# Attention and MLP in one launch: when two items' heads are loaded, and which PSUM banks the stages get

## The chip, the cores and the metric

The kernel runs on one core of one Trainium2 chip. The metric is the device time of one launch in microseconds, the median of several runs. A core has five engines that run side by side, each with its own queue of instructions, worked off in order: PE (TensorE, matrix products), DVE (VectorE), ACT (ScalarE), POOL (GpSimd) and SP (SyncE, which here issues every DMA). They wait for each other on semaphores. PE writes its products into PSUM, which has eight banks of 128 partitions by 512 float32 numbers.

## The reference

One transformer block on 2048 rows of width 512, float32:

```
x  = A_x                                          # 2048 x 512
qkv = layernorm(x) @ wqkv                         # 32 heads of 16 columns each
p  = softmax(q @ k^T / 4)                         # per head, 2048 x 2048
h  = x + (p @ v) @ wo
h2 = h + silu(layernorm(h) @ w1) @ w2             # inner width 1792
```

## The kernel before, in words

**Items.** Attention is cut into 32 items: item `i` is the block of 512 queries number `i // 8` with the four heads `4 * (i % 8)` and up, so the first eight items are all heads of the first 512 queries. For an item the four heads' keys (`ks`, all 2048) and queries (`qs`, the item's 512) lie in SBUF in one of `RING = 5` buffers. `load_k(i, k)` and `load_q(i, k)` (L196 to L205) each issue one DMA for one head, from the DRAM tensors `kd` and `qd`. `HEADS[k]` gives a head's place as a pair (a, j); half `j` of the partitions holds two heads.

**Maxima.** The softmax subtracts an upper bound of each row's maximum, which is computed exactly: `maximum` (L216) makes a 128 x 512 tile of scores on PE (`ps_m`) and DVE reduces it to 128 maxima (`mx`, L225). An item has 64 such tiles. `one_max` (L297) does the next one of the list: the halves `j` alternate, and within a half the first four tiles are of one head, the next four of the other. `burst(n)` does n of them. When an item's 64 are done, `finish_max` combines them on POOL, and three units later `place_max` (L254) turns the result on PE (`ps_n`), copies it on ACT (`mt`) and sends it by two DMAs into two rows of `qs`.

**Three stages and their banks.** `open_banks` (L133) opens PSUM pools; a bank of a newly opened pool that lies where banks of a closed pool lay is released by the last readers of the closed pool's tiles.

- Stage 0 (pools st of 3 banks and sm of 5): layer norm, the values of all rows, and queries and keys of the first two items. It ends with a burst of five maxima.
- Stage 1 (L578 to L607, pools st of 2 and sm of 6): the *late projections*, 24 units of 12 products each. `project_qk` (L406) makes 128 columns (eight heads, two items) of queries or keys for one block of 512 rows, in a bank of pool st. In the middle of the 12 products it calls a burst of six maxima, which use pool sm. Then ACT scales the bank into `scaled[b]` (in the profile `ks<-ps_qk`) and casts that to `sh` (three buffers), POOL makes the remainder `sl` (two buffers), and SP writes `sh` twice and `sl` once to `kd` or `qd`, in two DMAs. In the text the units have the code's number `n`, from -4 to 19. Units -4 to -1 are the keys of the third and fourth item (items 2 and 3), units 0 to 3 their queries; units 4 to 19 are those of items 4 to 7. The heads of items 2 and 3 are loaded in units 0 to 3. The last two units, 18 and 19, also start the first scores of attention (`begin_scores`) by the table `BESIDE_T`.
- Stage 2 (L611 on, pools st of 4, pv of 1, sm of 3): attention with the MLP of a finished block of rows between. Per group PE makes four tiles of scores (`ps_s`), ACT the exponentials (`pt`), PE the products with the values (`pv`), and up to three maxima of later items go beside them.

**What sets the order.** Every engine's order is the order of the calls (`keep_in_program_order`). SP is one queue for all DMAs: a DMA whose data isn't there, or whose buffer isn't free, holds up all behind it. The DMAs take eight semaphores in turn (called places here), so a DMA is issued only when the one eight before it has landed.

Of the kernel before, what the change touches and what calls it, by code (L numbers as in the profile page):

```python
# [77 lines left out]
def attention_mlp_kernel(ctx: ExitStack, tc: tile.TileContext, x, wqkv, wo, w1, w2, out):  # L78
# [25 lines left out]
    def dma(*a):  # L104
        pin(nc.sync.dma_start(*a))
# [27 lines left out]
    def open_banks(scope, n, **sizes):  # L133

        for kind, bufs in sizes.items():
            banks[kind] = scope.enter_context(tc.tile_pool(name=f"ps_{kind}{n}", bufs=bufs, space=PSUM))

    def bank(name, kind="st", dtype=F32):
        return banks[kind].tile([P, 512], dtype, tag=kind, name=name)
# [56 lines left out]
    def load_k(i, k, lo=0, n=S):  # L196
        a, j = HEADS[k]
        h = 4 * (i % 8) + 2 * a + j
        dma(ks[i % RING][64 * j:64 * j + 48, a, lo:lo + n], kd[:, h * DH:(h + 1) * DH, lo:lo + n])

    def load_q(i, k):
        a, j = HEADS[k]
        h = 4 * (i % 8) + 2 * a + j
        lo = i // 8 * 512
        dma(qs[i % RING][64 * j:64 * j + 48, a, :], qd[:, h * DH:(h + 1) * DH, lo:lo + 512])  # L205

    def fixed_rows(i):
        for j in range(2):
            r = 64 * j + 48
            dma(qs[i][r:r + 16], fix_q[:, None, :].to_broadcast([16, 2, 512]))  # L210
            dma(ks[i][r:r + 16].rearrange("p a (m n) -> p (a m) n", n=512),
                fix_k[:, None, :].to_broadcast([16, 8, 512]))
# [66 lines left out]
    def tick():  # L279
        at["step"] += 1  # L280
        for fn, a in agenda.pop(at["step"], ()):
            fn(*a)
# [14 lines left out]
    def one_max(half=None, ps=None):  # L297

        i = next_item()
        if i == ITEMS:  # L300
            return
        if half is None:
            half = at["half"]
            at["half"] = 1 - half
        if at["blocks"]:

            i = min(range(2), key=lambda n: (todo[n, half] or todo[n, 1 - half] or [(n, KC)])[0][1])
        elif not todo[i, half] and 64 * (i + 2) <= at["ready"] and KC * i - at["next"] > 12:

            i += 1  # L310
        half = half if todo[i, half] else 1 - half
        at["done"] += 1
        if maximum(*todo[i, half].pop(0), ps):
            steps = due_at(i)
            soon(steps, place_max, i, finish_max(i, at["group"] is not None and steps == WAIT))

    def burst(n, *more):
        for ps in more:
            one_max(ps=ps)
        for _ in range(n - len(more)):  # L320
            one_max()
# [16 lines left out]
    def scores(g, k, kind="st"):  # L338

        i, c = divmod(g, KC)  # L340
        a, j = HEADS[k]
        assert i in placed
        ps = bank("ps_s", kind)
        mm(ps, ks[i % RING][64 * j:64 * j + 64, a, c * P:(c + 1) * P], qs[i % RING][64 * j:64 * j + 64, a, :],
           start=True, stop=True)
        pts[g, k] = pt_tile("pt")
        act("activation", pts[g, k], ps, AF.Exp, scale=qk_f)


    with ExitStack() as pa:  # L350
# [55 lines left out]
        def project_qk(b, n, beside={}, scale=False):  # L406

            g, key = divmod(n, 2)
            cols = slice(key * D + g * P, key * D + (g + 1) * P)
            ps = bank("ps_qk")  # L410
            weave(product(ps, lambda c: wqk_h[:, c, cols], lambda c: wqk_l[:, c, cols],
                          lambda c: xth[b][:, c, :], lambda c: xtl[b][:, c, :], DC),
                  {k: n if callable(n) else (lambda n=n: burst(n)) for k, n in beside.items()})
            sh = xp.tile([P, 512], F16, name="sh")
            sl = xp.tile([P, 512], F16, name="sl", bufs=2)
            if scale:

                t = scaled[b]
                act("mul", t, ps, qk_s)
                act("copy", sh, t)  # L420
                pool("tensor_tensor", sl, t, sh, ALU.subtract)
            else:
                act("mul", sh, ps, qk_s)
                dve("scalar_tensor_tensor", sl, ps, qk_s, sh, op0=ALU.mult, op1=ALU.subtract)
            d = (kd if key else qd)[:, g * P:(g + 1) * P, b * 512:b * 512 + 512]
            hs, ls = (slice(0, 3, 2), 1) if key else (slice(0, 2), 2)
            dma(d[hs].rearrange("s d n -> d s n"), sh[:, None, :].to_broadcast([P, 2, 512]))
            dma(d[ls], sl)
# [152 lines left out]
        def begin_scores(n):  # L581

            for _ in range(n):
                g, k = first_scores.pop(0)
                scores(g, k, "sm")
                one_max(1 - HEADS[k][1])


        BESIDE_T = {3: lambda: begin_scores(3), 9: lambda: begin_scores(3)}, {3: lambda: (begin_scores(2), burst(2))}
        at["blocks"] = False  # L590
        open_banks(pa, 1, st=2, sm=6)

        pools.append(ctx.enter_context(tc.tile_pool(name="bp0", bufs=EARLY, side="right")))
        for g in range(1, NG // 2):
            for m, (b, key) in enumerate([(b, 1) for b in range(NB)] + [(b, 0) for b in range(NB)]):
                tick()
                if g == 1 and m < 2:
                    fixed_rows(2 + m)
                n = 8 * g + m - 12
                beside = {BESIDE_A1[m]: 6} if g == 1 and m < len(BESIDE_A1) else BESIDE_A  # L600
                if n >= 18:
                    beside = BESIDE_T[n - 18]
                project_qk(b, 2 * g + key, beside, True)
                if 0 <= n < 4:
                    for h in (n % 2 * 2, n % 2 * 2 + 1):
                        load_q(2 + n // 2, h)
                        load_k(2 + n // 2, h)  # L607

    open_banks(ctx, 2, st=4, pv=1, sm=3)  # L611
    pv = bank("pv", "pv")
    cpool = ctx.enter_context(tc.tile_pool(name="cpool", bufs=1, side="right"))
    bp = ctx.enter_context(tc.tile_pool(name="bp", bufs=PTS - EARLY))
# [369 lines left out]
    def maxima(g):  # L984

        i, c = divmod(g, KC)
        ready = min(ITEMS, i + RING - (0 if c == KC - 1 else 1)) * 64
        rate = max([(64 * (n + 1) - sum(x for x, m in zip(BESIDE, marks) if g <= m <= KC * n) - at["done"])
                    / max(1, KC * n - AHEAD - g) for n in range(i + 1, ITEMS)] or [0])
        if ready < END:  # L990
            rate = min(rate, (ready - at["done"]) / (KC - 1 - c or KC))
        at["due"] += max(0, rate)
        if g < LAG or g in marks or g - 1 in marks:

            return 0
        at["ready"] = ready
        most = 2 if c == JOINT and i and i - 1 not in FIRSTS else 3
        n = max(0, min(most, int(at["due"]), ready - at["done"]))
        at["due"] -= n
        return n  # L1000
# [3 lines left out]
    for g in range(groups):  # L1004
        tick()
        i, c = divmod(g, KC)
# [9 lines left out]
        if i in FIRSTS:  # L1016
            b, n = i // 8 - 1, c - OUTPUT
# [21 lines left out]
        n = maxima(g)  # L1039
# [48 lines left out]
```

## Time and profile before

| | us |
|---|---|
| median of 3 runs | 1687.23 (1686.25 to 1687.6) |
| the profiled execution | 1686.74 |
| its span, first to last instruction | 1685.0 |
| PE busy | 1661.9 (99%) |
| DVE busy | 1452.2 (86%) |
| ACT busy | 1240.0 (74%) |
| POOL busy | 283.8 (17%) |

Stage 0 ends near 95 us of the span, the late projections run from there to about 197 us, and attention and the MLP fill the rest. The page's busy share of PE counts overlapping instructions once, so 99% leaves some 23 us in which PE ran nothing. In rows of the timeline the columns are start, duration, engine, line, operation, output and input, shape and count; in brackets is the idle time before, with what ended it. Neighbouring instructions of one kind are merged, and the count is then over 1 (a merged row spans from its first start to its last end). Matmuls overlap: a 512-column product lasts 0.39 us in its row, while the next one starts 0.23 us after it.

### The profile page before, as it was taken

What the parts mean: (1) busy time and instruction counts of PE and PEld (TensorE: products, weight loads), DVE (VectorE), ACT (ScalarE), POOL (GpSimd) and SP (SyncE); (2) the same over time, 40 slices, a digit from 0 to 9 for tenths busy, and PEclk for the clock granted to TensorE, in tenths of its full rate; (3) what the DMA queues carried; (4) which work ended last, traced back from release to release, by engine and by line L of the source; (5) the groups of instructions that cost most, each with busy time, mean ns of one, the idle gap of its engine ahead of it and who ended that gap; (6) DMA issues with size and microseconds to landing.
All of it is one profiled execution on the core that took longest, in us unless ns stands there. A gap on an engine that the chain in (4) does not pass through costs nothing.

```text
span 1685.0 us, 28415 instructions
## 1 busy us (share of the span) xinstructions
PE 1661.9 (99%) x10542; PEld 650.2 (39%) x10542; DVE 1452.2 (86%) x2422; ACT 1240.0 (74%) x2441; POOL 283.8 (17%) x450
## 2 busy tenths in 40 slices
PE   9998999999999999999999999999999999999999
PEld 7665422222245532222245542222245542222387
DVE  7897999999978889999988889999978889997343
ACT  5322699999963279999963369999963379999743
POOL 5422310000033310000033310000034310000000
PEclk9999999999999999999999999999999999999999
DMA  5533411121223111111222211111222211100222
GB/s 179 125 87 129 120 43 39 37 50 38 64 59 88 60 49 32 37 49 39 62 60 80 69 50 31 37 45 43 60 61 80 70 49 32 35 11 21 64 75 82
DMA packets 100763, 102.83 MB, mean 61 GB/s; under 512 B 19092, under 2 KB 77524, under 8 KB 100624
## 3 DMA queue, kind: packets, MB, share of 16 engines
q1 hardware_dynamic: 100624, 101.01, 20.7%
q8 instruction: 83, 1.36, 0.3%
q14 instruction: 56, 0.46, 0.1%
HBM read 77.72 MB, written 17.29 MB: 56 GB/s over the span
## 4 chain that ended last, share of the span: by engine, by line
PE 85%; ACT 9%; DVE 3%; DMA 2%; issue 1%; POOL 0%; SPq 0%; ACTq 0%; DVEq 0%
PE pv L85 33%; PE ps_s L85 19%; PE ps_m L85 10%; PE ps_acc L85 10%; ACT pt L99 8%; PE ps_qk L85 4%; PE ps_wo L85 3%; PE ps_w L85 3%; PE ps_v L85 2%; DVE mx L225 1%; DMA ks<-kd 1%; PE ps_tr L88 1%; DMA ks<-in_A_x_dram 1%; DMA qd<-sh 0%; DVE pvs L102 0%
## 5 line engine op out<-in xcount | busy, mean ns | idle before, releaser
L225 DVE TENSOR_REDUCE mx<-ps_m 128x1 f32<-128x512 f32 x2009 | 1257.5, 682 | 92.6 <-PE ps_m L85 66.2
L99 ACT ACTIVATE pt<-ps_s 128x512 f32<-128x512 f32 x2048 | 1012.3, 608 | 19.0 <-PE ps_m L85 12.8
L85 PE MATMUL ps_s<-qs,ks 64*128 64x512 f16 x2048 | 534.0, 379 | 5.8 <-ACT pt L99 2.4
L85 PE MATMUL pv<-pt,va 128*17 128x512 f32 x4096 | 537.4, 598 | 1.2
L85 PE MATMUL ps_m<-ks,qs 48*128 48x512 f16 x2009 | 504.8, 380 | 6.2 <-ACT mt L99 3.2
L85 PEld LDWEIGHTS <-ks 64*128 64x128 f16 x2048 | 148.6, 94 | 542.2 <-issue 434.9
L85 PEld LDWEIGHTS pv<-pt,va 128*17 128x17 f32 x4096 | 68.7, 95 | 225.9 <-issue 208.3
L85 PEld LDWEIGHTS <-qs 48*128 48x128 f16 x2048 | 118.1, 94 | 73.9 <-issue 69.3
L99 ACT CAST w2h<-w 128x512 fp32r<-128x512 f32 x56 | 34.7, 620 | 102.0 <-PE ps_acc L85 102.0
L99 ACT ACTIVATE g<-pv 128x512 f32<-128x512 f32 x39 | 23.3, 597 | 102.2 <-PE pv L85 102.2
L85 PE MATMUL ps_acc<-w2l,gh 128*128 128x512 f32 x224 | 92.8, 415 | 0.0
L85 PE MATMUL ps_acc<-w2h,gh 128*128 128x512 f32 x224 | 92.4, 413 | 0.0
L85 PE MATMUL ps_acc<-w2h,gl 128*128 128x512 f32 x224 | 88.1, 393 | 0.0
L92 POOL TENSOR_TENSOR w2l<-w,w2h 128x512 fp32r<-128x512 f32 x42 | 53.8, 1281 | 164.7 <-ACT w2h L99 164.6
L102 DVE TENSOR_TENSOR gl<-g,gh 128x512 fp32r<-128x512 f32 x53 | 37.0, 699 | 46.7 <-ACT gh L99 46.7
L99 ACT ACTIVATE ks<-ps_qk,qk_s 128x512 f32<-128x512 f32 x30 | 20.7, 689 | 70.7 <-PE ps_qk L85 68.6
L92 POOL TENSOR_SCALAR nm<-nm 128x16 f32<-128x16 f32 x51 | 12.9, 253 | 327.1 <-DVE nm L235 323.8
L92 POOL TENSOR_TENSOR mx<-mx 128x32 f32<-128x32 f32 x38 | 9.5, 250 | 340.6 <-DVE mx L225 339.1
L85 PE MATMUL pv<-htl,w1h 128*128 128x512 f32 x156 | 65.6, 420 | 0.0
L92 POOL TENSOR_TENSOR ot<-ot,den 128x512 f32<-128x512 f32 (+1 forms) x16 | 20.4, 1273 | 256.3 <-DMA den<-dr 217.1
L85 PE MATMUL pv<-hth,w1h 128*128 128x512 f32 x156 | 62.5, 401 | 0.0
L85 PE MATMUL pv<-hth,w1l 128*128 128x512 f32 x156 | 61.4, 393 | 0.0
(130 smaller groups left out, 1409.4 us busy)
## 6 DMA issues: line engine op xcount, KB each, us to landing
w<-in_B_w_dram SPq DMA_DIRECT2D x112, 256.0 KB
ks<-kd SPq DMA_DIRECT2D x120, 192.0 KB
qs<-qd SPq DMA_DIRECT2D x128, 48.0 KB
kd<-sh SPq DMA_DIRECT2D x16, 256.0 KB
qd<-sh SPq DMA_DIRECT2D x16, 256.0 KB
hx<-in_A_x_dram SPq DMA_DIRECT2D x16, 256.0 KB
ot<-pvs SPq DMA_DIRECT2D x124, 32.0 KB
den<-dr SPq DMA_DIRECT2D x124, 32.0 KB
```

The lines of the kernel that those rows point to most:

```text
L85: tc.keep_in_program_order(nc.tensor.matmul(*a, **k))
L88: tc.keep_in_program_order(nc.tensor.transpose(*a))
L92: tc.keep_in_program_order(getattr(nc.gpsimd, op)(*a, **k))
L99: pin(getattr(nc.scalar, fn)(*a, **k))
L102: pin(getattr(nc.vector, fn)(*a, **k))
L225: pin(nc.vector.tensor_reduce(mx[i][:, j, a, qt, kb:kb + 1], ps, axis=AX.X, op=ALU.max))
```

## The change

Three edits, all in and around the late projections. `load_k` and `load_q` of items 2 and 3 are called in another order and in seven units in place of four. The pools of stage 1 are opened sm first, so sm takes banks 0 to 5 and st banks 6 and 7 (before: st 0 and 1, sm 2 to 7); those of stage 2 are opened st, sm, pv, so sm takes banks 4 to 6 and pv bank 7 (before: pv 4, sm 5 to 7). In the last unit the two scores and two maxima beside the products follow its first product in place of its third. Nothing is added or removed; PE, DVE, ACT and POOL keep their instructions and, but for those two products, their order.

```diff
+        loads = {0: ((load_k, 2, 0), (load_k, 2, 1)), 1: ((load_q, 2, 0), (load_q, 2, 1), (load_k, 2, 2)),
+                 2: ((load_q, 2, 2), (load_k, 2, 3), (load_q, 2, 3))}
+        for h in range(4):
+            loads[3 + h] = (load_k, 3, h), (load_q, 3, h)
+
-        BESIDE_T = {3: lambda: begin_scores(3), 9: lambda: begin_scores(3)}, {3: lambda: (begin_scores(2), burst(2))}
+        BESIDE_T = {3: lambda: begin_scores(3), 9: lambda: begin_scores(3)}, {1: lambda: (begin_scores(2), burst(2))}
         at["blocks"] = False
-        open_banks(pa, 1, st=2, sm=6)
+        open_banks(pa, 1, sm=6, st=2)
...
                 project_qk(b, 2 * g + key, beside, True)
-                if 0 <= n < 4:
-                    for h in (n % 2 * 2, n % 2 * 2 + 1):
-                        load_q(2 + n // 2, h)
-                        load_k(2 + n // 2, h)
+                for load, i, h in loads.get(n, ()):
+                    load(i, h)
...
-    open_banks(ctx, 2, st=4, pv=1, sm=3)
+    open_banks(ctx, 2, st=4, sm=3, pv=1)
```

SP's order around the loads, from the two programs, with `k2,0` for the keys of the third item's head with number 0 in `HEADS`, and `W(n)` for the two writes of unit n:

```
before: W(0) q2,0 k2,0 q2,1 k2,1 | W(1) q2,2 k2,2 q2,3 k2,3 mt mt | W(2) q3,0 k3,0 q3,1 k3,1 | W(3) q3,2 k3,2 q3,3 k3,3 | W(4) W(5) W(6) mt mt W(7)
after:  W(0) k2,0 k2,1 | W(1) q2,0 q2,1 k2,2 mt mt | W(2) q2,2 k2,3 q2,3 | W(3) k3,0 q3,0 | W(4) k3,1 q3,1 | W(5) k3,2 q3,2 | W(6) k3,3 q3,3 mt mt | W(7)
```

## The prediction

> **What bounds the kernel now.** I read the page's busy shares first, then the windows by stage, the waits, the timelines of PE, SP, ACT and DVE around the late projections, and the chain that ended last there.
>
> ```profile
> PE 1661.9 (99%) x10542; PEld 650.2 (39%) x10542; DVE 1452.2 (86%) x2422; ACT 1240.0 (74%) x2441; POOL 283.8 (17%) x450
> ```
>
> PE is the bound, so the change pays or costs where PE stands idle or runs slowly. Windows of 20 us show where that is (window, length, then busy time of PE, its weight loads, DVE, ACT, POOL, then granted clock, DMA share, GB/s):
>
> ```profile
> 100.00:120.00 20.00, 20.00 (x95) 12.30 (x94) 19.85 (x35) 7.31 (x12) 7.88 (x14) 1.00 0.45 115
> 120.00:140.00 20.00, 17.88 (x81) 11.26 (x80) 15.39 (x27) 5.79 (x10) 6.00 (x13) 0.91 0.27 95
> 140.00:160.00 20.00, 16.78 (x75) 10.73 (x73) 14.64 (x24) 5.39 (x9) 5.33 (x5) 0.91 0.40 141
> ```
>
> From 100 to 120 us PE and DVE are both full, so neither has room to hide a delay of the other. From 120 to 160 us PE loses 5.34 us and the clock falls to 0.91. PE's timeline has the bursts of maxima, one per unit (units 3 to 8 here, but for unit 6, whose burst is undisturbed), and what stood before them:
>
> ```profile
> 124.36 0.83 PE L85 MATMUL ps_m<-ks,qs 48*128 48x512 f16 x6
> 128.06 0.82 PE L85 MATMUL ps_m<-ks,qs 48*128 48x512 f16 x5
> 131.00 0.37 PE L85 MATMUL ps_m<-ks,qs 48*128 48x512 f16 x1 [2.12 <-DVE mx L225]
> 132.31 0.63 PE L85 MATMUL ps_qk<-xtl,wqk_h 128*128 128x512 f32 x1
> 132.74 0.63 PE L85 MATMUL ps_qk<-xth,wqk_h 128*128 128x512 f32 x1
> 135.85 0.82 PE L85 MATMUL ps_m<-ks,qs 48*128 48x512 f16 x6
> 143.65 0.61 PE L85 MATMUL ps_m<-ks,qs 48*128 48x512 f16 x4
> 147.48 0.39 PE L85 MATMUL ps_m<-ks,qs 48*128 48x512 f16 x2 [3.22 <-ACT mt L99]
> 152.33 0.82 PE L85 MATMUL ps_m<-ks,qs 48*128 48x512 f16 x6
> ```
>
> An undisturbed unit takes 3.70 us (124.36 to 128.06). Unit 4 to 5 takes 7.79, unit 7 to 8 takes 8.68: 4.09 and 4.98 lost, 9.07 us together. Each loss is a stall (2.12 and 3.22 us) and, after it, products that start 0.43 us apart (132.31 to 132.74).
>
> SP's timeline shows why. A DMA is issued when the one eight places before it has landed, so some issues mark landings:
>
> ```profile
> 117.92 0.33 SPq L105 DMA_DIRECT2D qd<-sl  x1
> 119.80 0.77 SPq L105 DMA_DIRECT2D qs<-qd  x1
> 126.61 1.26 SPq L105 DMA_DIRECT2D ks<-kd  x1
> 135.13 0.71 SPq L105 DMA_DIRECT2D ks<-kd  x1
> 138.36 0.67 SPq L105 DMA_DIRECT2D ks<-kd  x1
> 142.68 0.67 SPq L105 DMA_DIRECT2D ks<-kd  x1
> 145.95 0.34 SPq L105 DMA_DIRECT2D kd<-sl  x1
> ```
> ```profile
> 120.75 5.84 DMA ks<-kd
> 126.61 11.73 DMA ks<-kd
> 139.13 7.42 DMA qd<-sh
> ```
>
> In the chain, the load of keys k2,0 takes 5.84 us, k2,3 takes 11.73, and the write W(3) of unit 3 takes 7.42: one backlog. The stall of unit 4 ends at 131.0 when k2,1 has landed (DVE, the named releaser, had long been done); that of unit 7 when W(3) has landed at 146.55, since ACT's cast `sh` of unit 6 needs its buffer and the copy `mt`, whose bank the burst needs, stands behind the cast:
>
> ```profile
> 146.65 0.62 ACT L99 CAST sh<-ks 128x512 f16<-128x512 f32 x1 [3.96 <-DMA qd<-sh]
> ```
>
> **The loads.** Prices of the backlog, from the rows above: a pair of keys and queries 3.27 us (142.68, landing of k3,0, to 145.95, landing of k3,1), which by size (192 and 48 KB) is 2.62 and 0.65; two writes, a pair and the two `mt` 4.32 (138.36 to 142.68); two writes and a pair 4.13 (131.00 to 135.13), so two writes 0.86 and two `mt` 0.19. The second load of keys is dearer: 126.61 to 131.00 is 4.39, less 0.65 for q2,1 3.74.
>
> Sixteen loads and their instructions stay, so the backlog's content is unchanged; its order isn't. With PE undisturbed until then, k2,0 is issued right behind W(0)'s second write (117.92 + 0.33, near 118.3) and not behind that write's landing. It lands at 118.3 + 5.84 = 124.1, k2,1 at 127.9, W(1) at 128.7, q2,0 at 129.4, q2,1 at 130.0. Unit 4's sixth maximum needs k2,1 and q2,1 at 128.7: a stall of 1.3 in place of 2.12. Then k2,2 132.7, `mt` 132.9, W(2) 133.7, q2,2 134.4, k2,3 137.0, q2,3 137.7. The ninth tile of item 2, second in unit 6's burst, needs these; it would stand at 128.06 + 2 x 3.70 = 135.5. So both stalls together shift PE by 2.2 us. I take 2.2. Below, if the second keys cost 2.62 as later ones do, everything is 1.1 earlier and the shift is 1.1; above, the 9.07 of before.
>
> Behind W(3) the backlog now comes after the write and not before it: W(3) lands near 138.5, while unit 6, whose burst stands at 137.7 by now, has six products and a scale to go before its cast wants the buffer; so `mt` isn't late and the stall of unit 7 goes. What is late next: the writes of units 4 to 7 land 4.13 us apart, the casts come 3.70 apart, so the margin of some 2 us shrinks by 0.43 a unit and is just about used up at W(7), the last with a load ahead of it; a cast that came late there would delay no `mt` copy, as none stands there. POOL's remainders, with two buffers, come later still and wait for nothing that PE needs before unit 12. Item 3's heads are first needed in unit 15 (one tile in unit 4, then six a unit), past 170 us; with four times 0.86 + 3.27 behind 137.7 they land by 154. So the loads gain 9.07 - 2.2 = 6.9.
>
> **The first bank of stage 1.** Here the change adds a wait.
>
> ```profile
> 94.73 0.82 PE L85 MATMUL ps_m<-ks,qs 48*128 48x512 f16 x5
> 95.48 0.50 PE L85 MATMUL ps_qk<-xth,wqk_h 128*128 128x512 f32 x1
> 97.42 0.39 PE L85 MATMUL ps_qk<-xtl,wqk_h 128*128 128x512 f32 x1
> 97.65 0.39 PE L85 MATMUL ps_qk<-xth,wqk_h 128*128 128x512 f32 x1
> 98.29 0.82 PE L85 MATMUL ps_m<-ks,qs 48*128 48x512 f16 x6 [0.25 <-DVE mx L225]
> 101.78 1.08 PE L85 MATMUL ps_m<-ks,qs 48*128 48x512 f16 x6
> ```
> ```profile
> 94.42 3.82 DVE L225 TENSOR_REDUCE mx<-ps_m 128x1 f32<-128x512 f32 x6
> ```
>
> Before, unit -4's first product took a bank of the old st pool and waited for ACT's copy of values, long done: it starts at 95.48, ten products hide DVE's last reduces of stage 0 (to 94.42 + 3.82 = 98.24), and the burst waits only 0.25. Now st lies in banks 6 and 7, which the old sm pool held, and in the changed program this product waits for the last of those reduces, though the bank itself was reduced earlier. All of PE stands behind it: its start moves from 95.48 to 98.29, 2.81 later, less the 0.25 that the burst no longer waits: 2.56. DVE, emptied, has no work until that burst, and the window from 100 us shows no room to make it up.
>
> Does the clock fall too? PE would be idle from 94.73 + 0.82 to 98.29, 2.74 us. The windows around three idle stretches of before:
>
> ```profile
> 127.94:131.36 3.42, 1.30 (x8) 0.35 (x7) 3.39 (x6) 0.26 (x1) 0.00 (x0) 1.00 0.18 69
> 131.36:134.77 3.41, 3.41 (x9) 2.73 (x9) 0.81 (x2) 0.52 (x1) 2.41 (x7) 0.50 0.48 172
> 148.42:151.84 3.42, 3.42 (x10) 2.65 (x9) 0.76 (x2) 0.69 (x1) 0.00 (x0) 0.50 0.48 171
> 196.21:199.63 3.42, 2.64 (x20) 1.13 (x19) 2.35 (x5) 2.18 (x5) 1.01 (x2) 1.00 0.36 117
> ```
>
> After the stall of 2.12 us, in a window 38% busy, PE ran 3.41 us at 0.50; the 0.78 us near 198, 77% busy, brought nothing. 2.74 lies beyond the first, so I count a fall: eight products at 0.43 in place of 0.23 us, 1.6. Some of that PE lost anyway: the burst at 101.78 took 1.08 in place of 0.82, waiting for DVE, which a slower PE no longer does: 1.35. The wait costs 3.9; 2.56 without a fall, and if both stalls of 1.3 and 0.9 us in units 4 and 6 brought one each, 3.2 more. Below zero it can't go: an earlier start would need an earlier last reduce.
>
> The Trainium skill ("TensorE: Matmul & The Clock Gate", section "Why this matters for your kernels") advises no PE-idle gaps above about 3 us, as a window of idle drops the clock. By it a gap of 2.74 would keep the clock and the wait would cost 2.56; this trace differs, since 2.12 us was enough.
>
> **Banks of attention and the last unit.**
>
> ```profile
> 198.12 0.39 PE L85 MATMUL ps_s<-qs,ks 64*128 64x512 f16 x2 [0.78 <-ACT ks L99]
> ```
> ```profile
> 198.66 16.80 ACT L99 ACTIVATE pt<-ps_s 128x512 f32<-128x512 f32 x34
> ```
>
> Before, the first scores of stage 2 waited 0.78 for ACT to empty the last projection's bank. Now their bank was last read by a reduce or an exponential of the burst moved two products (0.46 us) up, which ends before the last product; instead the maxima behind and the clearing of `pv` wait for ACT. But ACT's exponentials still start at 198.66, behind the last unit's scale and cast, and run 34 in 16.80 us, 0.49 each, four to a group, as fast as PE's groups. So of the 0.78 little stays: 0.15, between 0 and 0.78. Elsewhere pools st, sm and pv have the sizes they had; I count nothing.
>
> **The sum**, against the profiled execution (1686.74, 0.49 below the median 1687.23): -9.07 + 2.2 + 3.9 - 0.15 = -3.1, so 1683.6 there and 1684.1 against the median. 0.2% is 3.4 us, about what a measurement of this kernel can tell from no change; the forecast lies just inside it.
>
> **Rivals.**
> - The clock falls in units 4 or 6 as well, or the stalls there are a little longer: +1.6 to +3.2, 1685.7 to 1687.3. For: the stalls are 1.3 and 0.9 us, above the harmless 0.78. Against: well below 2.12.
> - The clock doesn't fall at the first bank (the skill's rule): 2.56 in place of 3.9, 1682.7. For: its 2.74 us may lie across two windows. Against: 2.12 was enough.
> - The second keys cost what later ones do, 2.62: the stalls shrink to 1.1 together, 1683.0; with the rival above 1681.6. For: two loads of keys follow each other now. Against: the load behind the first was slow before, too.
> - Slower: the order doesn't relieve the queue, since the same sixteen loads pass it, units 4 and 7 lose their 9.07 as before, and the first bank's 3.9 comes on top, less 0.15: 1691.0. It decides from a remaining loss of 8.7 us on, when the time is 0.2% above before. Against: W(3) and W(2) stand ahead of eight loads that they followed.
> - The change does half: the stall of unit 7 stays (`mt` late for another reason), 4.98 - 0.9 us more than forecast, 1688.2. Against: the chain leads through W(3).
>
> **How the numbers follow.** Forecast 0.42 (1682.9 to 1685.3 by its bounds; 0.2% is at 1683.9, so 0.2 faster, 0.22 same); first rival 0.22, same; second and third 0.26, faster; fourth 0.06, slower; fifth 0.04, same. That makes 0.46 faster, 0.48 same, 0.06 slower. The range reaches from the second and third rival to the upper end of the first: 1681.2 to 1687.3; the fourth and fifth lie outside.
>
> **What would show it.** PE's first product of unit -4 starts at about 98.3, released by DVE, with a granted clock of 0.50 in the next 3 to 4 us. From there all is some 3.9 us later: unit 4's burst has its last maximum late by about 1.3 us, unit 6's is short of some 0.9, unit 7 has no wait for `mt`; the end of the late projections comes about 3 us earlier than before. The forecast is wrong if unit -4 starts on time, if the key loads land earlier or later than walked, or if attention's exponentials no longer follow each other in 0.49 us.

## The result, and the profile after

The changed kernel takes 1684.96 us (median of 17 runs, 1682.2 to 1687.62), the kernel before on the same chip 1687.66 (17 runs, 1686.25 to 1692.08). The ratio is 0.998, with a 95% interval of 0.9972 to 0.9987: 2.2 to 4.7 us faster. The profiled execution has a span of 1683.3 us against 1685.0. The forecast was 1684.1.

The page's busy shares of the changed kernel hide it, as those of before did:

```profile
PE 1662.1 (99%) x10542; PEld 650.1 (39%) x10542; DVE 1452.4 (86%) x2422; ACT 1239.6 (74%) x2441; POOL 284.0 (17%) x450
```

PE's timeline around the late projections of the changed kernel (bursts of stage 0's end and of units -4 and -3, then of units 4 to 8; in brackets the idle time and what ended it):

```profile
95.67 0.82 PE L85 MATMUL ps_m<-ks,qs 48*128 48x512 f16 x5
99.23 0.80 PE L85 MATMUL ps_qk<-xth,wqk_h 128*128 128x512 f32 x1 [2.74 <-DVE mx L225]
99.82 0.63 PE L85 MATMUL ps_qk<-xth,wqk_l 128*128 128x512 f32 x1
...
103.18 0.82 PE L85 MATMUL ps_m<-ks,qs 48*128 48x512 f16 x6
106.65 1.06 PE L85 MATMUL ps_m<-ks,qs 48*128 48x512 f16 x6
...
132.88 0.82 PE L85 MATMUL ps_m<-ks,qs 48*128 48x512 f16 x5
134.41 0.39 PE L85 MATMUL ps_m<-ks,qs 48*128 48x512 f16 x1 [0.71 <-DMA qs<-qd]
137.69 0.82 PE L85 MATMUL ps_m<-ks,qs 48*128 48x512 f16 x6
141.43 0.39 PE L85 MATMUL ps_m<-ks,qs 48*128 48x512 f16 x1
142.75 0.82 PE L85 MATMUL ps_m<-ks,qs 48*128 48x512 f16 x5 [0.93 <-DMA qs<-qd]
146.83 0.82 PE L85 MATMUL ps_m<-ks,qs 48*128 48x512 f16 x6
150.57 0.82 PE L85 MATMUL ps_m<-ks,qs 48*128 48x512 f16 x6
```

Two lengths sum it up, and they serve for every run below.

- **Entry**, from the start of stage 0's last burst to that of unit -4's: 7.51 us (95.67 to 103.18), before 3.56 (94.73 to 98.29), so 3.95 lost. PE's first product waits 2.74 us for DVE's last reduce of stage 0, and the next ones start 0.43 us apart.
- **Units 4 to 8**, from the start of unit 4's burst to that of unit 8's: 17.69 us (132.88 to 150.57), before 24.27 (128.06 to 152.33), so 6.58 gained. The two long stalls have become 0.71 and 0.93, both ended by the load of a head's queries; no wait for `mt` is left in unit 7.

Net -2.6 us. The spans differ by only 1.7, since in this execution stage 0's last burst came 0.94 us later than in the one of before (95.67 against 94.73). The change doesn't touch stage 0; the start of its last burst differs from execution to execution (94.37 to 98.97 us in the profiles here). In the latest of them the clock fell at 60 us; for the others the cause isn't shown. The windows of the changed kernel show where the clock fell and where not (window, length, busy time of PE, its weight loads, DVE, ACT, POOL, granted clock, DMA share, GB/s):

```profile
95.53:98.95 3.42, 0.95 (x6) 0.21 (x5) 3.36 (x6) 0.59 (x1) 0.00 (x0) 1.00 0.00 0
98.95:102.37 3.42, 3.14 (x7) 2.48 (x8) 0.22 (x1) 0.00 (x0) 0.00 (x0) 0.50 0.02 5
132.00:135.41 3.41, 2.70 (x14) 1.35 (x13) 3.38 (x7) 0.94 (x2) 1.15 (x1) 1.00 0.48 166
141.00:144.41 3.41, 2.48 (x13) 1.24 (x12) 2.72 (x6) 0.53 (x1) 0.60 (x1) 1.00 0.47 169
```

In this execution it fell once, after the entry's wait, for 3.42 us, and not in units 4 and 6. One such stretch takes 0.001 off a run's mean clock (half of 3.41 us in 1683). Of the 17 runs, four have a mean clock of 1.000 and took 1682.20 to 1682.96 us, so they had no whole stretch; seven have 0.999 (1683.39 to 1685.20), as the profiled one; two have 0.998; and four have 0.997 (1685.47 to 1686.70), more than one stretch. So the median stands for a mixture.

At the start of attention PE waits 0.45 us in place of 0.78, and ACT's exponentials follow its last scaling, which starts at 195.78, by 1.29 us (before 197.38 and 198.66: 1.28). PE and ACT of the changed kernel:

```profile
196.52 0.40 PE L85 MATMUL ps_m<-ks,qs 48*128 48x512 f16 x2 [0.45 <-ACT ks L99]
```
```profile
195.78 0.69 ACT L99 ACTIVATE ks<-ps_qk,qk_s 128x512 f32<-128x512 f32 x1 [1.26 <-PE ps_qk L85]
...
197.07 18.22 ACT L99 ACTIVATE pt<-ps_s 128x512 f32<-128x512 f32 x37
```

### The profile page after: what moved, and what is told of

Its sections match the earlier page's. It is cut to its first block, busy times and chain, and to the rows that moved or that the text cites. A ratio compares the mean times of both kernels' runs of the same rounds, so it can differ in the third digit from the quotient of the medians.

```text
span 1683.3 us, 28415 instructions
## 1 busy us (share of the span) xinstructions
PE 1662.1 (99%) x10542; PEld 650.1 (39%) x10542; DVE 1452.4 (86%) x2422; ACT 1239.6 (74%) x2441; POOL 284.0 (17%) x450
## 4 chain that ended last, share of the span: by engine, by line
PE 87%; ACT 9%; DVE 2%; DMA 1%; issue 1%; SPq 0%; POOL 0%; DVEq 0%; ACTq 0%
PE pv L85 33%; PE ps_s L85 19%; PE ps_m L85 10%; PE ps_acc L85 10%; ACT pt L99 8%; PE ps_qk L85 5%; PE ps_wo L85 3%; PE ps_w L85 3%; PE ps_v L85 2%; DVE mx L225 1%; PE ps_tr L88 1%; DMA qs<-qd 1%; DMA ks<-in_A_x_dram 0%; DVE pvs L102 0%; DMA va<-in_A_wqkv_dram 0%
```

## The experiments

Theory: the loads gain some 6.9 us and the first bank takes 3.9 back, of which 1.35 is the clock; the rest is nothing. The rivals give the gain to the banks, call the wait cheap (idle time only, or given back later), or expect the second stall to stay. Every kernel computes the whole reference; the eleven products of the `filler` kernels are extra and nothing reads them.

### The parts alone

`e1_loads`: the kernel before with the changed loads, all banks as before (the table `loads` is that of the change and left out here).

```diff
-                if 0 <= n < 4:
-                    for h in (n % 2 * 2, n % 2 * 2 + 1):
-                        load_q(2 + n // 2, h)
-                        load_k(2 + n // 2, h)
+                for load, i, h in loads.get(n, ()):
+                    load(i, h)
```

> The kernel before with the loads of items 2 and 3 as in the changed kernel, and all banks and the last unit as before. Three-part theory (loads gain, first bank of stage 1 costs, rest is nothing): units 4 to 8 lose 2.4 us in place of 9.07, so 6.7 us faster than before, ratio 0.996; unit -4 starts without a wait; the stalls are 0.7 and 0.9 us in units 4 and 6, none in unit 7. Rival, that the loads gain only what the whole change gained: 2.7 us faster, 0.998.

`e2_first_banks`: the kernel before with stage 1's pool sm opened first.

```diff
-        open_banks(pa, 1, st=2, sm=6)
+        open_banks(pa, 1, sm=6, st=2)
```

> The kernel before with stage 1's pools opened sm first, nothing else. Three-part theory: PE waits 2.7 us before unit -4's first product, runs 3.4 us at half clock behind it, and all later work is 3.9 us later: ratio 1.0023; the stalls of units 4 and 7 stay. Rival, that DVE's room or later slack takes the wait up: within 1 us of before, 1.000.

`e3_last_banks`: the kernel before with the pools of stage 2 and the last unit as changed.

```diff
-        BESIDE_T = ..., {3: lambda: (begin_scores(2), burst(2))}
+        BESIDE_T = ..., {1: lambda: (begin_scores(2), burst(2))}
-    open_banks(ctx, 2, st=4, pv=1, sm=3)
+    open_banks(ctx, 2, st=4, sm=3, pv=1)
```

> The kernel before with stage 2's pools opened st, sm, pv and the last unit's scores and maxima one product in, nothing else. Three-part theory: the wait of 0.78 us before the first scores shrinks, but ACT's exponentials start 1.28 us behind the last scaling as before, so 0 to 0.2 us faster: 1.000. Rival, that PE's wait there is on the path: 0.5 to 0.8 us faster, and the exponentials start that much earlier behind the last scaling.

These shared a chip and the runs of before (1688.02, 29 runs).

| | median us | ratio, 95% interval |
|---|---|---|
| e1_loads | 1680.77 (5 runs) | 0.9951 (0.9938 to 0.9964) |
| e2_first_banks | 1691.78 (12 runs) | 1.0016 (1.0007 to 1.0024) |
| e3_last_banks | 1687.92 (11 runs) | 0.9996 (0.9987 to 1.0005) |

By medians the loads gain 7.25 us, the first bank costs 3.8, the rest does nothing that can be measured; -7.25 + 3.8 - 0.1 is -3.6, and the whole change, on another chip, measured -2.7. The intervals are wide: by its ratio the first bank costs 1.2 to 4.1 us, which by itself doesn't tell 3.8 from the 2.5 of idle time alone. They allow both sums; the traces have to say what each part costs. PE's timeline of `e1_loads`, units 4 to 8:

```profile
128.51 0.82 PE L85 MATMUL ps_m<-ks,qs 48*128 48x512 f16 x5
130.55 0.39 PE L85 MATMUL ps_m<-ks,qs 48*128 48x512 f16 x1 [1.22 <-DMA qs<-qd]
...
137.56 0.39 PE L85 MATMUL ps_m<-ks,qs 48*128 48x512 f16 x1
138.19 0.82 PE L85 MATMUL ps_m<-ks,qs 48*128 48x512 f16 x5 [0.24 <-DMA qs<-qd]
...
146.01 0.82 PE L85 MATMUL ps_m<-ks,qs 48*128 48x512 f16 x6
```

17.50 us, as in the changed kernel. The sum of the stalls is the queue's; how it falls between units 4 and 6 depends on when PE arrives. PE of `e2_first_banks`:

```profile
99.37 0.50 PE L85 MATMUL ps_qk<-xth,wqk_h 128*128 128x512 f32 x1 [2.74 <-DVE mx L225]
...
135.97 0.37 PE L85 MATMUL ps_m<-ks,qs 48*128 48x512 f16 x1 [2.10 <-DVE mx L225]
...
152.42 0.61 PE L85 MATMUL ps_m<-ks,qs 48*128 48x512 f16 x2 [4.34 <-ACT mt L99]
...
204.27 0.40 PE L85 MATMUL ps_m<-ks,qs 48*128 48x512 f16 x2 [0.45 <-ACT ks L99]
```

The wait of 2.74 comes with this one edit (the entry is 7.31 us), and both stalls on the loads stay: the bank edit relieves no queue. Units 4 to 8 take 25.32 us here against 24.27 in before, with the same loads, since unit 7's stall was longer and the clock fell at other places; so the total of this run holds more than the first bank's wait. The last row was not expected. The wait at the start of attention is 0.45 here, where stage 2 is as before, and in `e3_last_banks`, where stage 2 is changed, it is still 0.78:

```profile
196.81 0.39 PE L85 MATMUL ps_s<-qs,ks 64*128 64x512 f16 x2 [0.78 <-ACT ks L99]
```

So it shrinks because stage 1 left the banks that stage 2's scores take, and not through stage 2's own edits.

### Which of the loads' edits counts

`e5_third_close`: banks as before, item 2 loaded as changed, item 3's eight loads in units 2 and 3. (Here and in `e6_by_need` the loop that reads the table is that of `e1_loads` and left out.)

```diff
+        loads = {0: ((load_k, 2, 0), (load_k, 2, 1)), 1: ((load_q, 2, 0), (load_q, 2, 1), (load_k, 2, 2)),
+                 2: ((load_q, 2, 2), (load_k, 2, 3), (load_q, 2, 3),
+                     (load_q, 3, 0), (load_k, 3, 0), (load_q, 3, 1), (load_k, 3, 1)),
+                 3: ((load_q, 3, 2), (load_k, 3, 2), (load_q, 3, 3), (load_k, 3, 3))}
```

> The kernel before with item 2's loads as in the changed kernel, but item 3's eight pairs in units 2 and 3 as before (in unit 2 behind item 2's last three). If the spread of item 3 is what removes the stall of unit 7: the write of unit 3 lands behind two more pairs (6.5 us later than in the kernel with all loads as changed), unit 6's cast and with it the copy mt is some 4.6 us late, and unit 7 stalls about 3.5 us, with a fall of the clock behind it up to 1.6 more: 3.5 to 5.1 us slower than the kernel with the changed loads alone, about 0.998 of before. Rival, that the order of item 2's loads is the whole gain: as fast as the changed loads alone, 0.995 to 0.996.

`e6_by_need`: banks as before; item 2's tiles of maxima are taken head by head, and each load stands one or two units ahead of its need.

```diff
+    for j in range(2):
+        todo[2, j].sort(key=lambda tile: tile[3])
+        loads = {0: ((load_k, 2, 1), (load_k, 2, 0)), 1: ((load_q, 2, 1), (load_q, 2, 0)),
+                 3: ((load_k, 2, 3), (load_q, 2, 3)), 4: ((load_k, 2, 2), (load_q, 2, 2))}
+        for h in range(4):
+            loads[5 + h] = (load_k, 3, h), (load_q, 3, h)
```

> The kernel before with its banks, and loads in the order in which they are needed: k2,1 k2,0 in unit 0, q2,1 q2,0 in unit 1, the other two heads of item 2 in units 3 and 4, item 3's heads in units 5 to 8; item 2's maxima are done head by head (16 tiles of a head before the half's other head, same tiles in all), so that two heads are needed only from unit 10 on. If the stalls are nothing but the landing of k2,1 with q2,1 and of k2,3 with q2,3: q2,1 lands 0.65 us earlier, the stall of unit 4 shrinks to about 0.5 us, unit 6 has none, and the time is 1.7 us better than with the changed loads alone: 8.4 us better than before by the trace's sum, ratio 0.994 to 0.995. If late maxima cost elsewhere: no better than the changed loads alone.

`e5_third_close` took 1685.78 us (11 runs), ratio 0.9992 (0.9983 to 1.0001), and `e6_by_need` 1678.92 (5 runs), 0.9951 (0.9937 to 0.9964), on one chip; before 1687.39 (21 runs). PE of `e5_third_close` in unit 7, and the window behind the stall:

```profile
145.17 0.39 PE L85 MATMUL ps_m<-ks,qs 48*128 48x512 f16 x2 [3.35 <-ACT mt L99]
```
```profile
146.36:149.77 3.41, 3.41 (x10) 2.51 (x8) 0.51 (x1) 0.69 (x1) 0.00 (x0) 0.50 0.47 169
```

With item 3's loads ahead of `W(3)` the second stall is back, with its half clock: units 4 to 8 take 22.34 us, 4.84 more than in `e1_loads`. That is the part of the change that took unit 7's stall away. By the medians, each against before beside it, it is 5.6 us, a little over the 3.5 to 5.1 expected. In `e6_by_need` units 4 to 8 take 15.76 us (128.66 to 144.42). One short wait for a load is left: unit 4's burst lasts 1.30 us in place of 0.82, as its last product waits for queries (the last row is of the waits from 128 to 130.5 us: total, times, longest):

```profile
128.66 1.30 PE L85 MATMUL ps_m<-ks,qs 48*128 48x512 f16 x6
...
136.58 0.82 PE L85 MATMUL ps_m<-ks,qs 48*128 48x512 f16 x6
140.68 0.82 PE L85 MATMUL ps_m<-ks,qs 48*128 48x512 f16 x6
144.42 0.82 PE L85 MATMUL ps_m<-ks,qs 48*128 48x512 f16 x6
```
```profile
PEld L85 <- DMA qs<-qd: 0.6, 1, 0.6
```

That wait costs 0.48 us by the unit's length (4.18 in place of 3.70), as expected. It is the fastest kernel here, ahead of both: some 8.5 us below before and 6 below the changed one.

### What the first bank's wait costs, and the clock's part in it

Eleven products that nothing reads, put before unit -4, fill the wait if their own bank is free. In `e4_filler` it was not: the bank was one of the new pool sm.

```diff
+        filler = bank("filler", "sm")
+        for _ in range(11):
+            mm(filler, wqk_h[:, 0, :P], xth[0][:, 0, :], start=True, stop=True)
```

> The changed kernel with eleven idle products (0.23 us each, written to a bank of pool sm that nobody reads) before unit -4, so that PE is busy through the wait; the wait itself stays. If the half clock follows from PE's idleness: unit -4's first product starts as before the edit, 2.8 us later than in the kernel before, the clock stays at 1.00, its burst comes 1.35 us earlier than in the changed kernel, and the whole is 1.3 us faster than the changed kernel: 0.9972. If the slow products behind the wait have another cause, they stay, and so does 0.998.

1688.25 us (11 runs), ratio 0.9995 (0.9986 to 1.0003), beside the first three. PE's timeline shows that the edit missed its aim, as the new pool waits for the old one as a whole. In the changed kernel the first product in a bank of the new st starts 0.06 us after stage 0's last reduce ends, here the first product in a bank of the new sm 0.15 us after it; the last reduced bank can lie under only one of the two pools. The products only came on top, and the clock fell all the same:

```profile
99.19 3.75 PE L85 MATMUL filler<-xth,wqk_h 128*128 128x512 f32 x11 [2.83 <-DVE mx L225]
```

`e7_filler_old_bank` takes a bank of stage 0's pool st, two lines earlier in the program:

```diff
+        filler = bank("filler", "st")
+        for _ in range(11):
+            mm(filler, wqk_h[:, 0, :P], xth[0][:, 0, :], start=True, stop=True)
         pb.close()
```

> The changed kernel with the eleven idle products again, now in a bank of stage 0's own pool st, which waits for nothing late. If the half clock follows from PE's idleness: PE is busy from the last burst of stage 0 to within 0.3 us of the reduce's end, unit -4's first product still starts 2.8 us later than in the kernel before, the clock stays at 1.00, unit -4's burst comes about 1.4 us earlier than in the changed kernel, and the whole is 1.3 us faster than that: 0.9972 of before. If the slow products have another cause, they stay.

1684.82 us (11 runs), ratio 0.998 (0.9971 to 0.9989), on the chip of `e5_third_close`. The entry is 6.06 us in place of 7.51, as expected, and the time is that of the changed kernel all the same. To see why, the same was run once more, and so was the pair with and without these products on the loads of `e6_by_need`, where hardly a stall on a load stands beside them (0.48 us there, 0.24 idle in `e8_need_first_banks`).

```diff
 e8_need_first_banks (against e6_by_need)
-        open_banks(pa, 1, st=2, sm=6)
+        open_banks(pa, 1, sm=6, st=2)
 e9_need_banks_filler (against e8_need_first_banks), and e12_filler_free_bank (against e6_by_need)
+        filler = bank("filler", "st")
+        for _ in range(11):
+            mm(filler, wqk_h[:, 0, :P], xth[0][:, 0, :], start=True, stop=True)
 e10_by_need_again is e6_by_need, e11_filler_again is e7_filler_old_bank
```

> The banks of before with the loads in the order of their need, and stage 1's pool sm opened first, so that its st lies in banks 6 and 7. There is no stall on a load left in the version without the bank edit (1678.9 us on its own chip), so the first bank's cost stands alone. My theory: 2.6 to 2.8 us of idle PE at unit -4 with the clock at 0.50 for 3.4 us behind it, 3.9 us by unit -3, nothing given back later, and 0.1 gained at the start of attention: 3.8 us over the same loads with the old banks, about 1682.7. Rival 'the wait costs only its idle time': 2.5 us over. Rival 'given back in attention': within 1 us. Where the wait pushes the loads' landings along with it, no new stall comes; a stall over 0.5 us in units 4 to 8 would speak against that.

> The same with eleven products, whose result nothing reads, in a bank of stage 0's pool st, which fill the wait of the first bank: PE stays busy, the wait itself stays. My theory (a fall of the clock is part of the price): the clock stays at 1.00, unit -4's first product comes no earlier, and the kernel is 1.3 us faster than without the filler products and 2.5 us slower than with the old banks. Rival 'the clock costs nothing here': the same time as without them. Rival 'something else in the filler kernel costs' (with the changed kernel's loads the run with these products was no faster, and a group at 464 us waited for POOL): again a wait of ACT for POOL's reciprocals near 464 us.

> The loads in the order of their need with the banks of before, once more, beside the two above on one chip: about 1679, 8.5 us below the kernel before, and the base of the two differences above. If chips or runs differ by more than the edits, this one lies over 1681.

> The changed kernel with the eleven products in stage 0's bank, once more. If the loss of 2.66 us at 462 to 494 us (ACT waiting 1.0 us for POOL) was chance, it isn't there now and the time is 1.3 us below the changed kernel's 1685.0, about 1683.7. If it belongs to the filler's timing, it comes back and the time is again about 1684.8.

> The loads in the order of their need and the banks of before, with the eleven products (nothing reads their result) at the end of stage 0. Here they fill no wait: PE doesn't stand idle at unit -4, so they cost their own 2.4 us (11 x 0.22). What is tested is where the three earlier kernels with these products lost 0.7 to 2.7 us near 462 us: there the small write of the denominators landed 3.6 to 4.1 us after its issue in place of 1.9 to 2.1, with a 16 KB packet of the instruction queue started 1.57 to 1.73 us behind the issue in place of 1.95 to 2.14. Theory 'eleven more PE instructions move the instruction fetch onto that write': the write takes 3.6 us or more here too, and the time is 1679 + 2.4 + 0.7 to 2.2, 1682.1 to 1683.6. Rival 'it comes from the changed banks': the write takes 2.0 us, and the time is 1681.5.

| | median us | ratio, 95% interval | entry | units 4 to 8 |
|---|---|---|---|---|
| e8_need_first_banks | 1682.95 (8 runs) | 0.9972 (0.9962 to 0.9983) | 7.58 | 15.92 |
| e9_need_banks_filler | 1682.64 (6 runs) | 0.9965 (0.9953 to 0.9977) | 6.06 | 15.85 |
| e10_by_need_again | 1679.16 (5 runs) | 0.9945 (0.9932 to 0.9959) | | |
| e11_filler_again | 1682.62 (6 runs) | 0.9969 (0.9957 to 0.9981) | 6.06 | 18.03 |
| e12_filler_free_bank | 1682.38 (6 runs) | 0.9968 (0.9955 to 0.998) | 6.14 | 15.70 |

(The first four on one chip with before at 1687.95, the last on another with before at 1688.2.)

The first bank alone costs 1682.95 - 1679.16 = 3.8 us, the number expected. The five runs of `e10_by_need_again` spread from 1678.07 to 1682.81, so it is the entry that tells it from the 2.5 us of idle time: 7.58 against 3.56, 4.0 lost. Nothing of it is given back: from attention's first exponential to the end of the span `e8_need_first_banks` takes 1486.3 us, `e10_by_need_again` 1486.5, before and the changed kernel 1486.3. PE and the window behind the wait of `e8_need_first_banks`, then PE of `e9_need_banks_filler` and its window there:

```profile
98.61 0.80 PE L85 MATMUL ps_qk<-xth,wqk_h 128*128 128x512 f32 x1 [2.74 <-DVE mx L225]
```
```profile
98.52:101.93 3.41, 3.32 (x8) 2.65 (x9) 0.03 (x1) 0.00 (x0) 0.00 (x0) 0.50 0.02 5
```
```profile
94.66 0.82 PE L85 MATMUL ps_m<-ks,qs 48*128 48x512 f16 x5
95.41 2.79 PE L85 MATMUL filler<-xth,wqk_h 128*128 128x512 f32 x11
98.22 0.50 PE L85 MATMUL ps_qk<-xth,wqk_h 128*128 128x512 f32 x1
100.72 0.82 PE L85 MATMUL ps_m<-ks,qs 48*128 48x512 f16 x6
```
```profile
98.08:101.49 3.41, 3.38 (x18) 2.03 (x17) 0.43 (x2) 0.00 (x0) 0.00 (x0) 1.00 0.00 0
```

Unit -4's first product stands 3.56 us behind the last burst in both (95.05 to 98.61, 94.66 to 98.22): the wait stays, and with PE kept busy the clock does too. Unit -4's burst is then 1.52 us earlier, so 1.5 of the entry's 4.0 us is the clock. Tile by tile, ACT's exponentials of `e9_need_banks_filler` run 2.00 us ahead of those of `e8_need_first_banks` (0.4 of it from the later stage 0 of the latter) up to 461 us of the span. There the lead shrinks by 0.71 and then by 1.51, and at the end nothing is left. The cause is in SP's timeline of the two, `e8_need_first_banks` first:

```profile
453.48 0.33 SPq L105 DMA_DIRECT2D dr<-rc  x1
455.53 2.56 SPq L105 DMA_DIRECT2D den<-dr  x4
```
```profile
451.44 0.33 SPq L105 DMA_DIRECT2D dr<-rc  x1
455.16 1.72 SPq L105 DMA_DIRECT2D den<-dr  x4
```

At the end of the first block of rows the reciprocals of the sums of the exponentials are written (`dr<-rc`, 8 KB) and read back spread out (`den<-dr`). The read waits for the write, POOL for the read, ACT for POOL and PE for ACT. The write lands 1.99 us after its issue in the one and 3.65 in the other. The chain that ended last of `e12_filler_free_bank`, where these products stand with the old banks, runs through it:

```profile
451.22 4.24 DMA dr<-rc
...
458.99 1.28 POOL ot L92
...
460.29 0.62 ACT oh L99
```

Of the write's 16 landings 15 come by 1.99 us and the last at 4.24. The one packet of the instruction queue near it (16 KB) starts 2.25 us after the write's issue and takes 0.96, until 3.21; the write's last eight packets of 64 bytes start from 3.20 to 3.29. In `e9_need_banks_filler` that packet runs from 1.58 to 2.62, and the eight start from 2.61 to 2.70. In all five kernels with the eleven products the write takes 3.65 to 4.24 us, in the nine without them, before and after among them, 1.90 to 2.08, and there the instruction packet starts 0.12 us or less before its end, or behind it.

The products aren't needed for such a delay. The first write of this kind, at 232 to 246 us, lands after 2.94 to 3.32 us in six kernels, none with the products, where a packet of code starts 0.88 to 0.97 us behind its issue; in the other eight, where none starts before 1.09 us, it lands after 1.41 to 1.45. `e6_by_need` (3.32) and `e10_by_need_again` (1.42) are one program. So a packet of code near the end of such a write goes with the delay, and in all five kernels with eleven more PE instructions it hit the write at 451 to 458 us. That costs 0.7 to 1.4 us at a place 365 us behind the products; in two of the profiles the clock fell there as well (1.5 us). That the packet and the late 512 bytes passed one DMA engine is inferred from these times, as the records name no engine, and why in `e12_filler_free_bank` the last eight packets hadn't started before 2.25 us, like the other 120, stays open. The Trainium skill ("Runtime: NRT & Kernel Launch", section "Instruction fetch mechanics") has code refilled in blocks of 16 KiB over a DMA queue of the engine's own, mostly hidden; the packet's size agrees, and here it was not hidden. Which engine's code it was, the records don't say.

So `e9_need_banks_filler` is no evidence against the clock's price: it gained it at the entry and lost as much elsewhere. `e11_filler_again` met neither of its two expected times: its write landed late again (4.03 us), but in its profile the clock held at 462 us, and its median is 2.2 us below that of `e7_filler_old_bank`, the same kernel on another chip. Five of its six runs have a mean clock of 1.000, of the eleven of `e7_filler_old_bank` four. A single total could not have told this.

## Why the prediction was right, point by point

- **The sum.** -3.1 was forecast. The medians give -2.7, the two profiles -2.6 without the start's 0.94. Of the 0.86 us between 1684.1 and 1684.96, 0.43 is that before itself measured 0.43 above the median that I started from.
- **The loads, -6.9.** -6.58 in the changed kernel, -6.77 in the trace of `e1_loads` and -7.25 by its times. The walk of the queue had the second keys 3.74 us behind the first (measured 3.52) and a remaining loss of 2.2: with 3.70 us for unit 4 to 5 and 4.10 for 6 to 7 (136.58 to 140.68 in `e6_by_need`), 4.81 and 5.40 lose 2.4. It was nearer on the sum than on its parts: unit 4 lost 1.1 us and not 1.3, unit 6 lost 1.3 and not 0.9. (The idle times 0.71 and 0.93 are shorter than these losses, since a product's row of 0.39 us still counts as busy when the next could have started.)
- **Unit 7's stall goes.** It did, and `e5_third_close` shows that item 3's loads behind `W(3)` are the reason: put back, 4.84 us are lost again. That refutes the fourth and fifth rivals.
- **The first bank, +3.9.** 3.95 in the trace, 3.8 by the medians of both pairs. This is the term that kept the change near no difference. The clock's share, 1.35, measured 1.4 to 1.5, but two errors met in it: six products and not eight started 0.43 us apart, and the burst of unit -3, which was to gain 0.26, still takes 1.06 us. That part is luck.
- **The clock.** The second rival (no fall at 2.74 us, 1682.7) failed in the profile: 0.50 from 98.95 to 102.37. Here the Trainium skill's rule of no PE-idle gap above about 3 us ("TensorE: Matmul & The Clock Gate", section "Why this matters for your kernels") would have kept the clock, and the measurement decides: the clock fell after 2.74 us in all three profiles with that wait. It did not in every run: the four of mean clock 1.000 took 1682.20 to 1682.96, which is this rival's time. The first rival (falls in units 4 and 6) failed in the profile too: those windows were 79% and 73% busy. But the four runs at 0.997, 1685.47 to 1686.70, lie about where it put them; where their clock fell isn't recorded. The forecast took one course for all runs, and the middle of the mixture came out near it.
- **The banks of attention and the last unit, -0.15.** Small, as said. The text saw that the scores would wait no more and the maxima behind them would (the row of 0.45 is `ps_m`), but took the moved burst as needed for it; `e2_first_banks` has the 0.45 without it and `e3_last_banks` keeps the 0.78 with it. Stage 1's new place frees the banks of stage 2's first scores. No time hangs on it, since ACT's exponentials start 1.28 to 1.29 us behind its last scaling either way.
- **The third rival** (second keys at 2.62 us) failed with 3.52.
- **A sign that missed.** The late projections were to end about 3 us earlier; ACT's last scaling starts 1.6 us earlier (195.78 against 197.38), 2.5 without the start's 0.94.

## What to carry to other kernels

Three edits that come as one can hide a loss of over half their gain: cost each at its own place, and test each alone. When a PSUM pool is opened over an old one, see who last reads the *whole* old pool and give the first product a bank whose readers are long done. Put a load in a serial queue by when it is needed, and look behind it: the write that it delays can stall an engine four units later.

## What the runs showed of the hardware that was not expected

**When the clock falls.** In the late projections the clock fell behind windows of 3.4 us in which PE was at most 42% busy (1.45 of 3.41 us in `e4_filler`). A longer stall than the one that brought a fall can bring none, if two windows share it. `e3_last_banks` shows both, a stall of 2.02 us and one of 3.27:

```profile
128.82:132.23 3.41, 1.39 (x6) 0.83 (x6) 3.41 (x6) 0.00 (x0) 0.25 (x1) 1.00 0.20 72
132.23:135.64 3.41, 3.41 (x10) 2.53 (x8) 0.08 (x1) 1.31 (x2) 2.80 (x9) 0.50 0.47 171
142.47:145.88 3.41, 1.82 (x10) 0.92 (x9) 3.00 (x6) 0.26 (x1) 0.00 (x0) 1.00 0.38 138
145.88:149.30 3.42, 1.74 (x8) 1.29 (x8) 2.00 (x4) 0.77 (x2) 1.15 (x1) 1.00 0.51 184
149.30:152.71 3.41, 3.41 (x19) 2.13 (x18) 1.45 (x3) 0.69 (x1) 0.00 (x0) 1.00 0.44 156
```

41% busy brought the half clock, 53% and 51% did not. But PE's busy share is not the whole rule: in `e9_need_banks_filler`, at the start of the block's output products, a window of 2.07 of 3.41 us (61%) was enough.

```profile
460.61:464.02 3.41, 2.07 (x13) 0.77 (x10) 2.33 (x4) 3.41 (x8) 2.13 (x2) 1.00 0.41 124
464.02:467.43 3.41, 3.41 (x10) 1.64 (x9) 0.60 (x1) 1.02 (x3) 0.41 (x1) 0.50 0.41 132
```

What the chip counts there stays open. Where these windows lie shifts from one execution to the next (the first full clock comes between 4.80 and 7.31 us of the span), so the same program's stalls cost differently: with the same loads units 4 to 8 took 24.27, 25.32 and 22.62 us in before, `e2_first_banks` and `e3_last_banks`. It is at least part of the spread of before, 1684.96 to 1691.85 in the 29 runs beside `e1_loads`: the fastest has the highest mean clock (0.999), and the three at 0.996 or less took 1689.45 to 1691.85. It isn't all of it, as those at 0.998 still run from 1686.52 to 1691.01.

**A fetch of code in the way of a small write.** With the same eleven products near 95 us a write some 360 us later landed 1.6 to 2.3 us late, as shown above. A kernel that differs only in its number of instructions need not run alike elsewhere.

**A backlog at three of sixteen places.** The trace notes the landing of a write in 16 steps. In before, 13 steps of the first write of W(3) come 1.9 to 2.5 us after its issue and the last three only after 6.7 to 7.4. The loads of keys and queries are late in just three steps as well: k2,0, issued at 120.75, has them at 126.05 to 126.59, and the one before them at 121.90. Their sources `kd` and `qd` have three blocks (3 x 512 x 2048). So the backlog of this kernel seems to stand at three of sixteen places, and the DMA share of 0.27 to 0.45 in the windows of before hides it. No run tried a load that is spread wider.
